# An attention and maxout kernel: loads and turns moved along a hand-written loop, and two output tiles moved ahead of a values step

## The chip, the core and the metric

The kernel runs on one core of one Trainium2 chip. The core has a matrix engine (TensorE, PE in the profile, with its weight loads shown as PEld), three other compute engines (VectorE is DVE, ScalarE is ACT, GpSimd is POOL), a queue engine (SyncE, SP) and 16 DMA engines. Each engine works through its own list of instructions in order and waits on semaphores for the others. The metric is the device time of one execution in microseconds (us).

## The reference

Two computations follow one another. The first is causal attention with 16 extra keys and values ("beacons") ahead of the sequence, for 8 batches, 8 heads, 576 tokens and head size 64. The second is a feed-forward layer that takes the largest of three products, on 4608 rows of 512.

```python
k_all = np.concatenate([beacon_k, k], axis=2)
v_all = np.concatenate([beacon_v, v], axis=2)
scores = scale * np.matmul(q, k_all.transpose(0, 1, 3, 2))
scores = np.where(causal, -1000000000.0, scores)
a = np.exp(scores - scores.max(-1, keepdims=True))
a /= a.sum(-1, keepdims=True) + 1e-09
attn_out = np.matmul(a, v_all)
x = attn_out.transpose(0, 2, 1, 3).reshape(B * S, H * D)
h = np.maximum(np.maximum(x @ w1, x @ w2), x @ w3)
out = h @ w_out
```

## The kernel before, in words

Attention is worked by pairs of heads, 32 pairs in all: four pairs to a batch, two pairs to a quad. For a pair, q and k are loaded in float32 into a staging tile `st` (eight buffers), cast to bf16 by POOL ("cast", L259), and turned so that the head dimension lies on partitions. From pair 14 on the turn is a DMA transpose, one for q and one for k ("cross", L378), into one of six pairs of tiles `qT` and `kT`; pairs before are turned by TensorE. "keys" copies the beacons' columns into `kT`. The values of a batch come in two pieces, loaded into `st` and cast into `v_sb`.

For each pair there are four groups of scores ("scores", L513): two or four matmuls into a PSUM tile, an exponential on ACT into `at_sb` (L522), and a causal mask on POOL ("mask", L541). When two pairs (a quad) are masked, a "values" step (L582) multiplies the weights with `v_sb` and with ones, for the first and for the second half of the tokens, 120 matmuls in all. ACT turns the sums into reciprocals ("invert", L603 and L605), DVE multiplies into `xT` ("multiply", L615), and POOL copies the other half into `xC` ("cross x", L680). A batch has two such values steps.

The feed-forward layer runs by blocks of tokens, one block to a batch after the first, one batch behind attention. A "unit" (L699) is 16 matmuls for one weight matrix and one slice of 128 hidden features. DVE takes the larger value into `hT` (L629, L631). "out" (L725) is the second layer for one or two tiles of 128 tokens, six matmuls a tile, with a copy to `y` by DVE (L733) and a store from SP (L759).

The order is a list of steps written out by hand (`first_steps`, `loop_steps`), which `emit_all` runs one after the other, so it is the order of every engine's instructions as well. In the loop one scores step and one unit alternate on TensorE, so that ACT and POOL work while units run. Four PSUM tiles, numbers 0 to 3, serve all steps; the last number of a step names its tile.

The step "load" takes the next entry of the list `loads` (pair loads and value pieces, in a fixed order) and issues its transfers from SP. With an engine's name it is gated: `load_pair` and `load_v` first let that engine write one column of the staging tile, so that the transfer waits until the engine has come to this place. All transfers of SP (loads, turns, stores) stand in one queue in program order.

```python
def next_load(n=1, gate=None):
    for _ in range(n):
        if loads:
            loads.pop(0)(*([idle[gate]] if gate else []))
```

Of the kernel before, what the change touches and what calls it, by code (L numbers as in the profile page):

```python
# [16 lines left out]
def kernel(  # L17
# [160 lines left out]
    def L(fn, *a):  # L178
        return lambda *more: fn(*a, *more)
# [656 lines left out]
    def start_late():  # L836
# [224 lines left out]
        ("load", 1, "pool"),  # L1061
        ("scores", 7, 3, 0),
        ("load", 1),
# [57 lines left out]
        ("cast", 12, "pool", "pool"),  # L1121
        ("load", 1),
        ("load", 1),
        ("scores", 9, 3, 0, 3),
        ("mask", 9, 3, "pool"),
        ("unit", 1),
        ("scores", 9, 1, 0, 0),
# [18 lines left out]
        ("cast", 14, "pool", "pool"),  # L1146
        ("cross", 14, 0),
        ("cross", 14, 1),
        ("load", 1),
        ("unit", 2),  # L1150
# [6 lines left out]
        ("cast keys 2", "pool"),  # L1157
        ("load", 1),
# [3 lines left out]
        ("cross keys",),  # L1162
        ("scores", 11, 2, 0, 0),
        ("mask", 11, 2, "pool"),
        ("unit", 1),
        ("scores", 11, 3, 0, 2),
# [4 lines left out]
        ("unit", 1),  # L1171
        ("unit", 2),
        ("cast", 15, "pool", "pool"),
        ("cross", 15, 0),
        ("cross", 15, 1),
        ("load", 1),
# [9 lines left out]
        ("cast", 16, "pool", "pool"),  # L1186
        ("cross", 16, 0),
        ("cross", 16, 1),
        ("load", 1),
# [6 lines left out]
        ("out", 2, 1),  # L1196
        ("store", 1),
        ("out", 1, 2),
        ("store", 1),
        ("scores", 12, 0, 0, 3),  # L1200
        ("mask", 12, 0, "pool"),
        ("unit", 0),
        ("load", 1),
        ("cast v", 3, 0, "pool"),
        ("scores", 12, 2, 0, 1),
        ("mask", 12, 2, "pool"),
        ("unit", 2),
        ("keys", 14, "act"),
        ("scores", 12, 3, 0, 3),
        ("mask", 12, 3, "pool"),  # L1210
        ("unit", 0),
        ("cast v", 3, 1, "pool"),
        ("scores", 12, 1, 0, 1),
        ("mask", 12, 1, "pool"),
        ("unit", 2),
        ("scores", 13, 0, 0, 3),
        ("mask", 13, 0, "pool"),
        ("unit", 0),
        ("cast", 17, "pool", "pool"),
        ("cross", 17, 0),  # L1220
        ("cross", 17, 1),
        ("load", 1),
        ("scores", 13, 2, 0, 1),
        ("mask", 13, 2, "pool"),
        ("unit", 2),
        ("keys", 15, "act"),
        ("scores", 13, 3, 0, 3),
        ("mask", 13, 3, "pool"),
        ("unit", 0),
        ("scores", 13, 1, 0, 1),  # L1230
        ("mask", 13, 1, "pool"),
        ("unit", 2),
        ("scores", 14, 0, 0, 3),
        ("mask", 14, 0, "pool"),
        ("unit", 0),
        ("cast", 18, "pool", "pool"),
        ("cross", 18, 0),
        ("cross", 18, 1),
        ("load", 1),
        ("scores", 14, 2, 0, 1),  # L1240
        ("mask", 14, 2, "pool"),
        ("unit", 2),
        ("keys", 16, "act"),
# [11 lines left out]
        ("unit", 3),  # L1255
        ("scores", 14, 1, 0, 2),
        ("mask", 14, 1, "pool"),
        ("unit", 0),
        ("cast", 19, "pool", "pool"),
        ("cross", 19, 0),  # L1260
        ("cross", 19, 1),
        ("load", 1),
# [3 lines left out]
        ("keys", 17, "act"),  # L1266
        ("scores", 15, 2, 0, 2),
        ("mask", 15, 2, "pool"),
        ("unit", 0),
        ("scores", 15, 3, 0, 1),  # L1270
# [5 lines left out]
        ("load", 1, "pool"),  # L1276
# [8 lines left out]
        ("cross x", 2, 1, 1, "pool"),  # L1285
        ("cast", 20, "pool", "pool"),
        ("cross", 20, 0),
        ("cross", 20, 1),
        ("load", 1),
        ("out", 2, 0),  # L1290
        ("store", 1),
        ("out", 2, 1),
        ("store", 1),
        ("scores", 16, 0, 0, 3),
        ("mask", 16, 0, "pool"),
        ("unit", 2),
        ("load", 1),
        ("cast v", 4, 0, "pool"),
        ("scores", 16, 2, 0, 0),
        ("mask", 16, 2, "pool"),  # L1300
        ("unit", 3),
        ("keys", 18, "act"),
        ("scores", 16, 3, 0, 1),
        ("mask", 16, 3, "pool"),
        ("unit", 2),
        ("cast v", 4, 1, "pool"),
        ("scores", 16, 1, 0, 0),
        ("mask", 16, 1, "pool"),
        ("unit", 3),
        ("scores", 17, 0, 0, 1),  # L1310
        ("mask", 17, 0, "pool"),
        ("unit", 2),
        ("cast", 21, "pool", "pool"),
        ("cross", 21, 0),
        ("cross", 21, 1),
        ("load", 1),
        ("scores", 17, 2, 0, 0),
        ("mask", 17, 2, "pool"),
        ("unit", 3),
        ("keys", 19, "act"),  # L1320
        ("scores", 17, 3, 0, 1),
        ("mask", 17, 3, "pool"),
        ("unit", 2),
        ("scores", 17, 1, 0, 0),
        ("mask", 17, 1, "pool"),
        ("unit", 3),
        ("scores", 18, 0, 0, 1),
        ("mask", 18, 0, "pool"),
        ("unit", 2),
        ("cast", 22, "pool", "pool"),  # L1330
        ("cross", 22, 0),
        ("cross", 22, 1),
        ("load", 1),
        ("scores", 18, 2, 0, 0),
        ("mask", 18, 2, "pool"),
        ("unit", 3),
        ("keys", 20, "act"),
        ("values", 8, 0, 1),
# [7 lines left out]
        ("unit", 0),  # L1346
        ("scores", 18, 3, 0, 3),
        ("mask", 18, 3, "pool"),
        ("unit", 1),
        ("scores", 18, 1, 0, 3),  # L1350
        ("mask", 18, 1, "pool"),
        ("unit", 2),
        ("cast", 23, "pool", "pool"),
        ("cross", 23, 0),
        ("cross", 23, 1),
        ("load", 1),
        ("scores", 19, 0, 0, 0),
        ("mask", 19, 0, "pool"),
        ("unit", 1),
        ("keys", 21, "act"),  # L1360
        ("scores", 19, 2, 0, 3),
        ("mask", 19, 2, "pool"),
        ("unit", 2),
        ("scores", 19, 3, 0, 0),
        ("mask", 19, 3, "pool"),
        ("unit", 1),
        ("scores", 19, 1, 0, 3),
        ("mask", 19, 1, "pool"),
        ("unit", 2),
        ("load", 1, "pool"),  # L1370
        ("unit", 0),
        ("values", 9, 0, 1),
        ("invert",),
        ("values", 9, 1, 3),
# [5 lines left out]
        ("cast", 24, "pool", "pool"),  # L1380
        ("cross", 24, 0),
        ("cross", 24, 1),
        ("load", 1),
        ("out", 2, 2),
        ("store", 1),
        ("out", 2, 0),
# [5 lines left out]
        ("unit", 2),  # L1392
        ("load", 1),
        ("cast v", 5, 0, "pool"),
        ("scores", 20, 2, 0, 0),
        ("mask", 20, 2, "pool"),
        ("unit", 1),
        ("keys", 22, "act"),
        ("scores", 20, 3, 0, 3),
        ("mask", 20, 3, "pool"),  # L1400
        ("unit", 2),
        ("cast v", 5, 1, "pool"),
        ("scores", 20, 1, 0, 0),
# [4 lines left out]
        ("unit", 2),  # L1408
        ("cast", 25, "pool", "pool"),
        ("cross", 25, 0),  # L1410
        ("cross", 25, 1),
        ("load", 1),
        ("scores", 21, 2, 0, 0),
        ("mask", 21, 2, "pool"),
        ("unit", 1),
        ("keys", 23, "act"),
        ("scores", 21, 3, 0, 3),
        ("mask", 21, 3, "pool"),
        ("unit", 2),
        ("scores", 21, 1, 0, 0),  # L1420
# [4 lines left out]
        ("unit", 2),  # L1425
        ("cast", 26, "pool", "pool"),
        ("cross", 26, 0),
        ("cross", 26, 1),
        ("load", 1),
        ("scores", 22, 2, 0, 0),  # L1430
        ("mask", 22, 2, "pool"),
        ("unit", 1),
        ("keys", 24, "act"),
        ("values", 10, 0, 3),
# [6 lines left out]
        ("cross x", 4, 0, 1, "pool"),  # L1441
        ("unit", 0),
        ("scores", 22, 3, 0, 1),
        ("mask", 22, 3, "pool"),
        ("unit", 3),
        ("scores", 22, 1, 0, 1),
        ("mask", 22, 1, "pool"),
        ("unit", 2),
        ("cast", 27, "pool", "pool"),
        ("cross", 27, 0),  # L1450
        ("cross", 27, 1),
        ("load", 1),
        ("scores", 23, 0, 0, 0),
        ("mask", 23, 0, "pool"),
        ("unit", 3),
        ("keys", 25, "act"),
        ("scores", 23, 2, 0, 1),
        ("mask", 23, 2, "pool"),
        ("unit", 2),
        ("scores", 23, 3, 0, 0),  # L1460
        ("mask", 23, 3, "pool"),
        ("unit", 3),
        ("scores", 23, 1, 0, 1),
        ("mask", 23, 1, "pool"),
        ("unit", 2),
        ("load", 1, "pool"),
        ("unit", 0),
        ("values", 11, 0, 3),
        ("invert",),
        ("values", 11, 1, 1),  # L1470
# [4 lines left out]
        ("cross x", 4, 1, 1, "pool"),  # L1475
        ("cast", 28, "pool", "pool"),
        ("cross", 28, 0),
        ("cross", 28, 1),
        ("load", 1),
        ("out", 2, 2),  # L1480
        ("store", 1),
        ("out", 2, 0),
        ("store", 1),
        ("scores", 24, 0, 0, 3),
        ("mask", 24, 0, "pool"),
        ("unit", 1),
        ("load", 1),
        ("cast v", 6, 0, "pool"),
        ("scores", 24, 2, 0, 2),
        ("mask", 24, 2, "pool"),  # L1490
        ("unit", 3),
        ("keys", 26, "act"),
        ("scores", 24, 3, 0, 0),
        ("mask", 24, 3, "pool"),
        ("unit", 1),
        ("cast v", 6, 1, "pool"),
        ("scores", 24, 1, 0, 2),
        ("mask", 24, 1, "pool"),
        ("unit", 3),
        ("scores", 25, 0, 0, 0),  # L1500
        ("mask", 25, 0, "pool"),
        ("unit", 1),
        ("cast", 29, "pool", "pool"),
        ("cross", 29, 0),
# [206 lines left out]
```

## Time and profile before

| | |
|---|---|
| median of 3 runs | 290.99 us |
| the three runs | 288.12, 295.52, 290.99 us |
| the profiled execution | 288.71 us |
| its span (first to last instruction of the program) | 286.9 us |
| TensorE's granted clock over the span | 1.00 |
| HBM read and written | 35.13 MB, 9.44 MB |
| transfers by hardware queues (q1) | 39.20 MB, 72.8% of the 16 DMA engines' time |
| POOL cast of a pair's q or k (x44) | 822 ns each |
| DVE copy of two output tiles (x20, some of one tile) | 1090 ns each |

The profile is of one execution. "Busy" is the time in which an engine worked, and "idle before" the time that it stood ahead of a group of instructions, with what ended that idle time. The chain of waits follows the end of the program back, at each step to what released it. "Issue" there is time in which an engine waited for nothing that the profile shows.

### The profile page before, as it was taken

The numbers are of one execution on the slowest core, as the hardware profiler recorded it, in microseconds if no ns is written. First come the engines' busy times: TensorE is split into PE (matmuls) and PEld (weight loads), VectorE is DVE, ScalarE is ACT, GpSimd is POOL, SyncE is SP. The second block draws the span as 40 slices with busy tenths as digits, with TensorE's granted clock in tenths as the row PEclk, the third lists the DMA queues.
The fourth block names the chain that finished last, engine by engine and source line by source line (L and its number), as shares of the span: only waits on it lengthen the run. The fifth ranks groups of instructions, "written<-read, shape, count | busy, mean of one in ns | idle before, by whom it ended". The sixth has DMA issues, their size and how long they took to land.

```text
span 286.9 us, 11693 instructions
## 1 busy us (share of the span) xinstructions
PE 275.5 (96%) x5099; PEld 204.3 (71%) x5099; DVE 177.1 (62%) x331; ACT 155.1 (54%) x249; POOL 140.6 (49%) x280
## 2 busy tenths in 40 slices
PE   7999999899899999999999998989999999999995
PEld 6656777667677577876888476866888478867762
DVE  2455878866566665756666565645666565761654
ACT  3886676877363367734765176624765186624000
POOL 4562228898763187626763396616763173400000
PEclk9999999999999999999999999999999999999999
DMA  9999999989999989889999999899999220003004
GB/s 156 177 166 210 219 238 159 244 198 218 231 185 159 148 167 305 133 156 177 192 218 163 158 162 295 138 185 164 242 214 141 78 110 5 2 3 148 2 2 183
DMA packets 118307, 46.27 MB, mean 161 GB/s; under 512 B 107248, under 2 KB 112880, under 8 KB 118256
## 3 DMA queue, kind: packets, MB, share of 16 engines
q1 hardware_dynamic: 111888, 39.20, 72.8%
q0 software_dynamic: 5808, 6.00, 13.3%
q8 instruction: 40, 0.66, 1.1%
q10 hardware_dynamic: 560, 0.33, 0.4%
q14 instruction: 11, 0.09, 0.1%
HBM read 35.13 MB, written 9.44 MB: 155 GB/s over the span
## 4 chain that ended last, share of the span: by engine, by line
PE 87%; DMA 4%; ACT 3%; issue 2%; POOL 1%; DVE 1%; ACTq 0%; POOLq 0%
PE t L699 44%; PE t L725 16%; PE t L582 11%; PE t L513 6%; DMA quad<-in_k_dram 2%; ACT at_sb L522 2%; PE pv L637 2%; DMA bk<-in_beacon_k_dram 2%; PE sc L513 1%; PE sc L637 1%; PE fps L637 1%; PE t L397 1%; POOL at_sb L541 1%; PE wide L582 1%; PE pv L582 1%
## 5 line engine op out<-in xcount | busy, mean ns | idle before, releaser
L699 PE MATMUL t<-xT,w_sb 64*128 64x288 bf16 (+1 forms) x1008 | 130.5, 285 | 0.9 <-issue 0.9
L699 PE MATMUL t<-xC,wC 64*128 64x288 bf16 (+1 forms) x1008 | 130.3, 285 | 0.0
L522 ACT ACTIVATE at_sb<-t 128x992 bf16<-128x992 f32 (+1 forms) x96 | 82.7, 863 | 54.4 <-PE t L513 46.4
L541 POOL TENSOR_SCALAR_AFFINE_SELECT at_sb<-at_sb 128x256 bf16<-128x256 bf16 (+2 forms) x143 | 53.3, 389 | 61.2 <-ACT at_sb L522 46.4
L631 DVE TENSOR_TENSOR hT<-hT,t 128x576 bf16<-128x576 bf16 (+1 forms) x84 | 63.7, 762 | 31.3 <-PE t L699 31.3
L699 PEld LDWEIGHTS <-w_sb 64*128 64x128 bf16 x1008 | 52.7, 94 | 12.8 <-issue 2.1
L699 PEld LDWEIGHTS <-wC 64*128 64x128 bf16 x1008 | 52.7, 94 | 11.3
L725 PE MATMUL t<-w_out_sb,hT 128*128 128x512 bf16 x210 | 46.9, 380 | 0.0
L259 POOL CAST p<-st 96x768 bf16<-96x768 f32 x44 | 35.0, 822 | 8.0 <-DMA qT<-p 7.4
L629 DVE CAST hT<-t 128x576 bf16<-128x576 f32 (+1 forms) x36 | 27.7, 769 | 15.2 <-PE t L699 15.0
L615 DVE TENSOR_TENSOR xT<-t,recip 128x288 bf16<-128x288 f32 (+2 forms) x78 | 23.0, 351 | 22.6 <-ACT recip L605 18.9
L725 PEld LDWEIGHTS <-hT 128*128 128x128 bf16 x210 | 19.9, 98 | 23.3 <-issue 0.2
L680 POOL COPY xC<-xT 64x576 bf16<-64x576 bf16 (+1 forms) x26 | 18.2, 699 | 36.1 <-DVE xT L615 35.9
L513 PE MATMUL t<-qT,kT 64*128 64x288 bf16 (+4 forms) x288 | 33.4, 279 | 0.0
L733 DVE COPY y<-t 128x1024 f32<-128x1024 f32 (+1 forms) x20 | 21.8, 1090 | 17.1 <-PE t L725 16.8
L582 PEld LDWEIGHTS <-v_sb 128*32 128x32 bf16 (+1 forms) x1408 | 24.8, 96 | 5.4 <-issue 4.2
L582 PE MATMUL t<-at_sb,v_sb 128*32 128x96 bf16 (+8 forms) x1144 | 24.0, 228 | 3.2 <-issue 3.2
L513 PEld LDWEIGHTS <-kT 64*128 64x128 bf16 x400 | 18.8, 94 | 10.7 <-issue 6.3
L603 ACT ACTIVATE lnd<-t 128x288 f32<-128x288 f32 x26 | 10.7, 410 | 28.7 <-PE t L582 28.7
L522 ACT ACTIVATE at_sb<-sc 128x736 bf16<-128x736 f32 (+5 forms) x28 | 23.2, 862 | 4.3 <-PE sc L513 4.1
L315 POOL CAST v_sb<-st 128x1536 bf16<-128x1536 f32 (+2 forms) x21 | 18.4, 894 | 0.0
L637 PEld LDWEIGHTS <-w_sb 128*128 128x128 bf16 x144 | 13.1, 98 | 3.3 <-issue 1.4
(125 smaller groups left out, 214.2 us busy)
## 6 DMA issues: line engine op xcount, KB each, us to landing
out_dram<-y SPq DMA_DIRECT2D x15, 512.0 KB, 5.3
st<-in_q_dram SPq DMA_DIRECT2D x24, 288.0 KB, 5.8
st<-in_k_dram SPq DMA_DIRECT2D x24, 288.0 KB, 6.6
st<-in_v_dram SPq DMA_DIRECT2D x24, 256.0 KB, 5.4
w_sb<-in_moe_w_dram POOLq DMA_DIRECT2D x6, 384.0 KB, 8.4
st<-in_v_dram SPq DMA_DIRECT2D x8, 224.0 KB, 4.9
st<-in_v_dram SPq DMA_DIRECT2D x8, 160.0 KB, 5.2
out_dram<-y SPq DMA_DIRECT2D x5, 256.0 KB, 2.7
```

The costliest lines, as they stand in the source:

```text
L259: cast(t16.rearrange("p r h d -> p h r d"), st[0:QP, i * NQ2 : (i + 1) * NQ2].rearrange("p (h r d) -> p h r d", h=2, r=QR),)
L513: nc.tensor.matmul(ps[:, e, off : off + q1 - q0], kT[hs, 128 * t : 128 * t + 128], qT[hs, q0:q1], start=True, stop=True, tile_position=(64 ...
L522: nc.scalar.activation(out=both_heads(p, gi), in_=ps[:, :, 0 : g_width(p, gi)], func=AF.Exp, scale=scale)
L541: nc.gpsimd.affine_select(out=view, in_=view, compare_op=ALU.is_ge, fill=0.0, base=x0, pattern=[[0, 2], [1, hi - lo]], channel_multiplier=-1,)
L582: nc.tensor.matmul(ps[bank][32 * j : 32 * j + 32, lo + q0 - qa : lo + qb - qa], lhsT, at_view(PPQ * quad + j // 2, t, j % 2, q0, qb), star ...
L615: nc.vector.tensor_mul(xT[:, 2 * g + part - 1, c0 + ca : c0 + cb], ps[bank][:, lo : lo + cb - ca], recip[:, ca:cb],)
L629: (by_i or by_dve)(h, ps)
L631: nc.vector.tensor_max(h, h, ps)
L637: nc.tensor.matmul(ps[:, f], w_in[i][:, ct, 128 * (ft + f) : 128 * (ft + f + 1)], xT[:, ct, lo : lo + MID], start=(ct == 0), stop=(ct == n ...
L699: nc.tensor.matmul(ps[:, e], w[own(e), ct, cols], x, start=(ct == 0 and not over), stop=(ct == n_ct - 1 and over), tile_position=(64 * e, 0),)
L725: nc.tensor.matmul(ps[:, u], h_tile(tt + u, ft), w_out_sb[:, ft, :], start=(ft == 0), stop=(ft == n_ft - 1),)
L733: nc.vector.tensor_copy(y[:, 0:n], ps[:, 0:n])
```

## The change

No instruction of the computation is added or taken away. Three things move.

The order of `loads` changes: the pair loads of a batch follow that batch's value pieces, where they ran one pair further ahead.

```diff
     loads = load_pairs(10, 12) + load_v_pieces(2) + load_pairs(12, 16)
-    loads += [L(load_beacons, B_PE, B, bk32)] + load_pairs(16, 17)
+    loads.append(L(load_beacons, B_PE, B, bk32))
     for b in range(3, B):
-        loads += load_v_pieces(b) + load_pairs(PPB * b + 5, min(PPB * b + 9, NPAIR))
+        loads += load_v_pieces(b) + load_pairs(PPB * (b + 1), min(PPB * (b + 2), NPAIR))
```

The steps "load", "cast" and "cross" stand at other places. Two loads leave `first_steps` and come later in the loop; casts and turns come two to three pairs ahead of their scores, where they came four to five ahead; most loads are gated by POOL (16 more small fills there). "cast v" comes one pair later, and the cast of the beacons and its turn move a few steps.

Of the four or five output tiles of a block, which stood behind the batch's second values step, two now stand just ahead of the next batch's first values step. The PSUM tile numbers of most steps change with it. This is the batch of pairs 16 to 19, from the end of the batch ahead (mask steps and all of the lines between are left out where "..." stands):

```diff
         ("values", 7, 1, 2),
         ...
         ("cross x", 2, 1, 1, "pool"),
-        ("cast", 20, "pool", "pool"),
-        ("cross", 20, 0),
-        ("cross", 20, 1),
-        ("load", 1),
-        ("out", 2, 0),
-        ("store", 1),
-        ("out", 2, 1),
-        ("store", 1),
-        ("scores", 16, 0, 0, 3),
-        ("unit", 2),
-        ("load", 1),
-        ("cast v", 4, 0, "pool"),
-        ("scores", 16, 2, 0, 0),
-        ...
-        ("scores", 17, 0, 0, 1),
-        ("unit", 2),
-        ("cast", 21, "pool", "pool"),
-        ...
-        ("scores", 18, 0, 0, 1),
-        ("unit", 2),
-        ("cast", 22, "pool", "pool"),
-        ...
-        ("scores", 18, 2, 0, 0),
-        ("unit", 3),
-        ("keys", 20, "act"),
-        ("values", 8, 0, 1),
+        ("cast", 18, "pool", "pool"),
+        ("cross", 18, 0),
+        ("cross", 18, 1),
+        ("load", 1, None),
+        ("out", 2, 0),
+        ("store", 1),
+        ("scores", 16, 0, 0, 1),
+        ("unit", 3),
+        ("scores", 16, 2, 0, 2),
+        ("unit", 1),
+        ("cast", 19, "pool", "pool"),
+        ("cross", 19, 0),
+        ("cross", 19, 1),
+        ("load", 1, None),
+        ...
+        ("scores", 17, 0, 0, 0),
+        ("unit", 3),
+        ("cast v", 4, 0, "pool"),
+        ("scores", 17, 2, 0, 2),
+        ("unit", 1),
+        ("load", 1, "pool"),
+        ...
+        ("scores", 18, 0, 0, 0),
+        ("unit", 3),
+        ("cast", 20, "pool", "pool"),
+        ("cross", 20, 0),
+        ("cross", 20, 1),
+        ("load", 1, "pool"),
+        ("keys", 19, "act"),
+        ("scores", 18, 2, 0, 2),
+        ("unit", 1),
+        ("out", 2, 0),
+        ("store", 1),
+        ("values", 8, 0, 3),
```

More of the change, by code (lines that the diff above doesn't have):

```diff
@@ L1171 @@
         ("unit", 1),
+        ("load", 1, "pool"),
         ("unit", 2),
[L1173 to L1176, printed above, removed]
+        ("cross keys",),
         ("unit", 3),
@@ L1195 @@
         ("store", 1),
-        ("out", 2, 1),
+        ("out", 1, 1),
         ("store", 1),
-        ("out", 1, 2),
-        ("store", 1),
[L1200 to L1206, printed above, removed]
-        ("unit", 2),
[L1208 to L1212, printed above, removed]
@@ L1230 @@
[L1230 to L1243, printed above, removed]
+        ("scores", 12, 0, 0, 2),
+        ("mask", 12, 0, "pool"),
+        ("unit", 3),
@@ L1244 @@
+        ("cross", 16, 1),
+        ("load", 1, "pool"),
+        ("keys", 15, "act"),
+        ("scores", 14, 2, 0, 0),
+        ("mask", 14, 2, "pool"),
+        ("unit", 1),
+        ("out", 2, 2),
+        ("store", 1),
         ("values", 6, 0, 3),
```

532 lines of the change are left out of this document (271 added, 261 removed).

## The prediction

> **What bounds the kernel now.** I read the page's shares first, then the chain of waits in order of time, then the busy time by windows. On the page:
>
> ```profile
> span 286.9 us, 11693 instructions
> ...
> PE 275.5 (96%) x5099; PEld 204.3 (71%) x5099; DVE 177.1 (62%) x331; ACT 155.1 (54%) x249; POOL 140.6 (49%) x280
> ...
> DMA  9999999989999989889999999899999220003004
> ...
> q8 instruction: 40, 0.66, 1.1%
> ```
>
> TensorE is busy for 275.5 of 286.9 us, and no other engine exceeds 62%. DMA is busy nine tenths of every slice up to about 226 us, so it is the resource with the least room, but nothing waits for it unless TensorE does. Whatever the change gives must therefore be TensorE idle time. The chain of waits (start, length, what; "issue" is time in which nothing that the profile shows was waited for) says where that is after the first 56 us:
>
> ```profile
> 56.09 0.91 issue
> ...
> 77.11 1.28 issue
> ...
> 126.45 5.29 PE t L725 x24
> 131.74 0.32 PE t L513 x4
> 132.05 0.98 PE t L699 x16
> ...
> 140.27 0.98 PE t L699 x16
> ...
> 143.62 2.29 PE t L582 x120
> ...
> 157.17 6.58 PE t L725 x30
> ...
> 175.48 2.29 PE t L582 x120
> 177.77 0.71 PE t L699 x9
> 178.48 0.91 issue
> ...
> 190.22 1.01 issue
> ```
>
> From 56 us on there are four holes, 0.91 + 1.28 + 0.91 + 1.01 = 4.1 us. All lie in or just behind a values step (L582, 120 matmuls in 2.29 us), and no engine or transfer ends them. To see what they have in common I counted TensorE's work between them, with windows cut inside the holes (columns: width, then busy us and instructions of PE, PEld, DVE, ACT, POOL, clock, DMA share, GB/s):
>
> ```profile
> 56.50:77.80 21.30, 20.12 (x383) 13.88 (x383) 14.00 (x22) 14.47 (x24) 17.49 (x25) 1.00 1.10 206
> 77.80:178.90 101.10, 100.09 (x1916) 74.75 (x1915) 63.42 (x105) 55.79 (x90) 58.66 (x112) 1.00 1.05 189
> 178.90:190.70 11.80, 10.83 (x255) 9.37 (x256) 7.70 (x14) 5.91 (x9) 4.85 (x12) 1.00 1.10 147
> ```
>
> Matmuls plus weight loads are 766, 3831 and 511: nearly 3, 15 and 2 times 256 (instructions that only wait are not counted). The page has 40 instruction packets, 0.66 MB, for 2 x 5099 TensorE instructions: 255 instructions a packet. So a packet holds 256 instructions and the holes stand at packet limits. A values step uses 240 instructions in 2.29 us, a first-layer unit (L699) 32 in 0.98 us, four second-layer output tiles (L725) 48 in 5.29 us, so two tiles 24 in 2.64 us. A values step eats nearly a packet in 2.29 us; where the packet limits lie at its two ends, the next packet comes too late. That is my reading of the holes, an inference from counts.
>
> [...]
>
> **The change, part by part.** The sum is made on the profiled execution: 288.71 us, of which 286.9 is span and 1.8 lies around it.
>
> *TensorE's work* is the same: both programs have 5099 matmuls. 0 us.
>
> *Gates.* 16 loads get a tiny fill on POOL ahead of them. The fills there are now (busy us, mean ns, idle before):
>
> ```profile
> L202 POOL MEMSET st<- 96x1 f32 x6 | 0.6, 106 | 0.1
> ```
>
> 16 x 0.106 = 1.7 us on an engine that is 49% busy and that TensorE doesn't wait for: 0 us, 1.7 if that cover were gone. The load behind a gate waits until POOL gets there, and SP with it; queued behind it on SP are the next turn, which waits for a later POOL cast anyway, and the next store, for whose tile there are four buffers.
>
> *Output tiles moved from behind a second values step.* They covered the chain from a values step to the first unit of the next block (reciprocal, multiply, copy into xC). Its last link, and the cast that follows it, on POOL:
>
> ```profile
> 128.49 0.66 POOL L680 COPY xC<-xT 64x576 bf16<-64x576 bf16 x1 [0.89 <-DVE xT L615]
> 129.22 1.59 POOL L259 CAST p<-st 96x768 bf16<-96x768 f32 x2
> ```
>
> The copy ends at 129.15, 2.70 us behind the values step (ended 126.45). With four tiles the first unit stood at 132.05. With two it stands at 126.45 + 2.64 + 0.32 = 129.41, still 0.26 us later than the copy, and only its second half, 0.49 us on, reads that copy. So 0 us; if the copy slipped by a whole microsecond, 1.0 - 0.75 = 0.25 us in each of seven blocks, 1.8 us.
>
> *The same tiles ahead of a first values step* give ACT and POOL 2.64 us more for masks that nobody waits for now: 0 us. They also shift packet limits. Counting instructions in the two programs, the packets of the last two holes hold the same as before: 119 values matmuls then, 120 now; 118 then and now. So these holes can shrink only by faster packets. One packet that was nearly as tight, over the values step at 143.62 (97 values matmuls), gets 12 output matmuls in place of 11 of the units': 2.64 - 11 x 0.98/16 = 2.0 us more room.
>
> *Loads and turns moved.* Two pair loads leave the stretch ahead of 77.11; I take half off that hole (bounds: all 1.28, or nothing). The hole at 56.09 stands ahead of all edits and stays; 178.48 falls in a stretch whose new neighbours (a turn, a V load, a store) are as heavy as its old ones and stays at 0.91; at 190.22 the V load moves away, and I take half of 1.01. Gain 0.64 + 0.50 = 1.1 us, at best 4.1 - 0.9 = 3.2. At worst a loss: the last two holes grow to the longest seen, 1.28, and the two packets that hold 81 and 86 values matmuls and pass now get one each: 0.4 + 0.3 + 2 x 1.28 = 3.2 us. I stay near the rows of the four holes, as DMA stays busy.
>
> What is late next is the turn, cast two to three pairs ahead where it was four to five. For pair 18, cast just behind a second values step: cast at 129.22 as in the row above; its scores stand behind two output tiles and eight steps of scores and unit, 126.45 + 2.64 + (140.27 + 0.98 - 131.74) = 138.6. That is 9.4 us. What a turn takes (casts on POOL, issues on SP, then median us from issue to landing):
>
> ```profile
> 108.01 1.59 POOL L259 CAST p<-st 96x768 bf16<-96x768 f32 x2
> ...
> 112.50 3.28 SPq L378 DMA_TRANSPOSE qT<-p  x1
> 115.89 2.02 SPq L378 DMA_TRANSPOSE kT<-p  x1
> ...
> 128.72 1.22 SPq L378 DMA_TRANSPOSE kT<-p  x1
> ```
>
> ```profile
> qT<-p SPq DMA_TRANSPOSE x16, 5.0
> kT<-p SPq DMA_TRANSPOSE x16, 3.8
> ```
>
> Undelayed: cast to 130.81, the second issue some 1.3 us after the first, so 132.1 + 3.8 = 135.9, 2.7 us to spare. The slowest quoted: cast at 108.01, landed 115.89 + 3.8 = 119.7, 11.7 us, as its first issue came 2.9 us behind the cast's end, held up on SP by earlier transfers; that would be 2.3 us late. In the new order only one pair load, gated some four units earlier, stands ahead of such a turn on SP, so I take the undelayed value: 0 us. Behind a late turn, SP holds the next load and store, and TensorE, in order, everything.
>
> Sum: 288.7 - 1.1 = 287.6. The three timed runs lie at 288.12, 290.99 and 295.52, the profiled one 2.3 us under their median. A scatter of 7 us from waits on a full DMA should partly stay: I put back 1.2 of the 2.3 us, an estimate without a row, and forecast 288.8.
>
> **The rivals.** *A: no packet comes faster.* For: the last turn moves behind seven units with their scores, a values step and three output tiles, 7 x (140.27 + 0.98 - 131.74)/8 + 2.29 + 3.96 = 14.6 us, so the same bytes get 14.6 us more room in some 226, and DMA stays nearly full. The holes stay at 4.1 us. Time: 288.7 to 291.0. [...] Chance 0.20.
>
> *B: the spread works everywhere.* The three holes behind 56.09 close (3.2 us) and the runs lose their scatter: 285.5; with the first hole as well 284.6, the floor, as nothing else from 56 us on is idle. For: where DMA is at 0 to 2 tenths, behind 230 us, no hole stands in a values step. Against: the unmoved counts of the last two packets. Chance 0.23.
>
> *C, slower: turns come late.* Pairs 18, 22, 26 and 30 are cast behind second values steps; each has 9.4 us, or 10.7 where a third tile stands there (22, 30). At the slow turn's 11.7 us TensorE stands 2 x 2.3 + 2 x 1.0 = 6.6 us. It decides from a landing 9.4 us behind the cast. 287.6 + 6.6 = 294.2, and with the median's 2.3 us 296.5. For: DMA is full, and the 16 turns' medians hide such cases. Against: SP's queue ahead of these turns is shorter. Chance 0.15.
>
> Forecast, partly closed holes and no new wait: 0.42.
>
> **How the numbers follow.** The time is the likeliest case's, 288.8, whose own range is 286.5 to 291. The whole range takes in B's floor, 284.6, and most of C, up to 294.5. About 2% is what this kernel's runs can tell from no change, 285.2 to 296.8. Faster: B's lower part and the edge of the forecast, 0.22. Slower: C with a bad median, or C with new holes (3.2 us), 0.13. The rest, 0.65.
>
> **What would show it.** In the changed profile the chain should have TensorE's steps back to back from 56 us on, with "issue" holes only in or behind values steps and multiples of 256 instructions apart; the one near 178 us should be there still. Two tiles after a second values step must be followed by scores and unit with no gap. A gap ahead of scores ended by the transfer of qT or kT is C, and makes the prediction wrong; so do more than four holes, or none.

## The result, and the profile after

| | kernel before | changed kernel |
|---|---|---|
| median | 289.54 us (22 runs, 287.30 to 295.52) | 287.55 us (22 runs, 286.11 to 290.53) |
| the profiled execution | 288.71 us | 289.68 us |
| ratio | | 0.9936, 95% interval 0.9915 to 0.9957 |

The change makes the kernel 0.6% faster, 2.0 us by the medians. The ratios here and below leave out the runs that are more than 1.5% above the fastest of the same kernel, while the medians and the counts of runs take in all. The profiled execution of the changed kernel is one of its slowest, so its profile tells where time can go and not what the median gained. A second profile of the same kernel, taken later beside other kernels, is of 288.82 us.

The page of the changed kernel, the lines that answer to those shown of before:

```profile
span 287.9 us, 11732 instructions
...
PE 277.3 (96%) x5099; PEld 204.6 (71%) x5099; DVE 177.2 (62%) x331; ACT 155.0 (54%) x249; POOL 142.9 (50%) x296
...
DMA  9999997999979299999999999997999551003004
...
q8 instruction: 40, 0.66, 1.0%
```

The same 5099 matmuls and 40 packets; POOL is 2.3 us busier; DMA is at seven tenths or more in all slices up to 223 us but one, and at five tenths or less behind. The chain of waits of the changed kernel (start, length, what):

```profile
60.30 2.76 PE t L725 x12
...
76.70 1.78 PE t L582 x83
78.54 0.70 PE t L582 x37
...
126.70 2.70 PE t L725 x12
...
129.72 0.98 PE t L699 x16
...
141.28 2.70 PE t L725 x12
...
155.24 1.86 PE t L582 x86
157.22 0.68 PE t L582 x31
...
176.32 2.29 PE t L582 x120
178.61 1.09 PE t L699 x16
...
187.58 2.28 PE t L582 x116
189.86 1.26 issue
...
213.77 0.71 issue
...
284.68 0.36 DVE y L751
```

A hole inside a step shows as two rows of that step whose times don't meet: 76.70 + 1.78 = 78.48 against 78.54, so 0.06 us where 1.28 us stood before; 155.24 + 1.86 = 157.10 against 157.22, so 0.12 us, new. The hole that stood at 178.48 is gone (176.32 + 2.29 = 178.61). The one at 190 is there and longer, 1.26 us, and there is a new one at 213.77, 0.71 us. From the first pair of output tiles at 60.30 on that is 2.15 us, where the kernel before has 1.28 + 0.91 + 1.01 = 3.20 us.

The same rows at the two ends, in the chain of the kernel before and in that of the second profile of the changed kernel:

```profile
59.00 2.70 PE t L725 x12
...
283.69 0.36 DVE y L751
```

```profile
59.44 2.69 PE t L725 x12
...
188.91 1.27 issue
...
212.84 0.76 issue
...
283.80 0.36 DVE y L751
```

From the first tiles to the last copy the kernel before takes 283.69 - 59.00 = 224.69 us, the changed one 224.38 and 224.36 us. So in the profiled executions the holes give 1.0 us and the whole stretch gives only 0.3. Most of the other 0.7 us is the price of taking a step of output tiles apart: 24 matmuls in 5.29 us before, 2 x 2.70 us now, which is 0.11 us in each of the five blocks that are split, 0.55 us. The run with little DMA traffic shows the same 0.11 us below.

None of this is 2 us. A part of that gain must lie in executions of the kernel before that are not its profiled one; the last two experiments bear on it.

### The profile page after: what moved, and what is told of

Its sections match the earlier page's. It is cut to its first block, busy times and chain, and to the rows that moved or that the text cites. A ratio compares the mean times of both kernels' runs of the same rounds, so it can differ in the third digit from the quotient of the medians.

```text
span 287.9 us, 11732 instructions
## 1 busy us (share of the span) xinstructions
PE 277.3 (96%) x5099; PEld 204.6 (71%) x5099; DVE 177.2 (62%) x331; ACT 155.0 (54%) x249; POOL 142.9 (50%) x296
## 4 chain that ended last, share of the span: by engine, by line
PE 85%; DMA 7%; issue 4%; POOL 1%; DVE 1%; POOLq 0%; DVEq 0%
PE t L699 44%; PE t L725 16%; PE t L582 10%; PE t L513 6%; DMA w_out_sb<-in_moe_w_out_dram 5%; DMA st<-in_v_dram 3%; PE pv L477 2%; PE pv L582 1%; PE sc L513 1%; PE t L397 1%; PE fps L637 1%; POOL at_sb L541 1%; PE sc L477 1%; POOL v_sb L315 1%; PE fps L582 0%
## 5 line engine op out<-in xcount | busy, mean ns | idle before, releaser
L541 POOL TENSOR_SCALAR_AFFINE_SELECT at_sb<-at_sb 128x256 bf16<-128x256 bf16 (+2 forms) x143 | 54.3, 396 | 51.3 <-ACT at_sb L522 42.3
L699 PEld LDWEIGHTS <-wC 64*128 64x128 bf16 x1008 | 52.1, 94 | 11.4
L725 PE MATMUL t<-w_out_sb,hT 128*128 128x512 bf16 x210 | 47.7, 380 | 0.1
L582 PEld LDWEIGHTS <-ones 128*32 128x32 bf16 (+2 forms) x512 | 11.0, 95 | 7.3 <-issue 4.4
```

Of the source, the lines that this page charges most:

```text
L541: nc.gpsimd.affine_select(out=view, in_=view, compare_op=ALU.is_ge, fill=0.0, base=x0, pattern=[[0, 2], [1, hi - lo]], channel_multiplier=-1,)
L582: nc.tensor.matmul(ps[bank][32 * j : 32 * j + 32, lo + q0 - qa : lo + qb - qa], lhsT, at_view(PPQ * quad + j // 2, t, j % 2, q0, qb), star ...
L699: nc.tensor.matmul(ps[:, e], w[own(e), ct, cols], x, start=(ct == 0 and not over), stop=(ct == n_ct - 1 and over), tile_position=(64 * e, 0),)
L725: nc.tensor.matmul(ps[:, u], h_tile(tt + u, ft), w_out_sb[:, ft, :], start=(ft == 0), stop=(ft == n_ft - 1),)
```

## The experiments

My theory: TensorE loses time where a packet of 256 instructions comes too late behind a dense values step, and the change moves some packets. The first rival: the holes have nothing to do with packet limits. The second: one part of the change does all of it. Each ratio below is to the kernel before on the same chip in the same session, with its 95% interval.

**One part alone: the tiles.** The output tiles stand as in the changed kernel; loads, casts, turns and the list of loads are as before.

```diff
-    loads.append(L(load_beacons, B_PE, B, bk32))
+    loads += [L(load_beacons, B_PE, B, bk32)] + load_pairs(16, 17)
     for b in range(3, B):
-        loads += load_v_pieces(b) + load_pairs(PPB * (b + 1), min(PPB * (b + 2), NPAIR))
+        loads += load_v_pieces(b) + load_pairs(PPB * b + 5, min(PPB * b + 9, NPAIR))
```

> Only the output tiles move (with the PSUM tile numbers that go with it); loads, casts and turns keep their old places. Packet theory: two output tiles (12 matmuls in 2.70 us) ahead of a first values step let TensorE's queue reach the packet limit long before the values matmuls run, so the next packet is there in time. Expected: no hole at the values step near 176 us, the hole near 190 us stays (about 1 us), the hole near 77 us stays (its two loads are back); ratio to the kernel before 0.994 to 0.997. Rival, spread of DMA: the gain comes from loads and turns, so this kernel stays at 0.999 to 1.001 with all four holes.

Measured: 0.9957 (0.9922 to 0.9992). The profiled execution, of 290.93 us, gives the most telling trace of the study. Its chain of waits, and its busy time by windows (columns: width, then busy us and instructions of PE, PEld, DVE, ACT and POOL, the granted clock, DMA share, GB/s):

```profile
77.52 2.44 issue
79.95 1.19 PE t L582 x36
```

```profile
80.00:82.00 2.00, 2.00 (x45) 1.41 (x46) 0.00 (x0) 0.79 (x3) 0.00 (x0) 0.50 0.79 240
82.00:84.00 2.00, 2.00 (x26) 1.28 (x24) 1.39 (x4) 0.89 (x2) 0.89 (x2) 0.75 0.81 181
84.00:90.00 6.00, 6.00 (x94) 4.22 (x92) 3.96 (x6) 3.67 (x5) 4.10 (x9) 1.00 1.47 191
```

The hole in the values step at 77 us is here 2.44 us long, and behind it the granted clock is 0.50, then 0.75, then 1.00 again. A late packet was thus paid twice here, by the hole and by slow matmuls behind it: 36 of the values step took 1.19 us, where 37 took 0.70 us in the changed kernel (the row at 78.54). This execution's mean clock is 0.994, and so is that of three more of this kernel's 12 runs. At 178 us there is no hole, and the one near 190 us stays (0.93 us at 192.31), both as expected. By the medians of all runs, 288.39 and 289.16 us, the ratio is 0.997, at the upper end of what was expected.

**The other part alone: loads and turns.** They stand as in the changed kernel, the tiles as before.

```diff
         ("out", 2, 0),
         ("store", 1),
-        ("scores", 16, 0, 0, 1),
+        ("out", 2, 1),
+        ("store", 1),
+        ("scores", 16, 0, 0, 3),
...
-        ("out", 2, 0),
-        ("store", 1),
-        ("values", 8, 0, 3),
+        ("values", 8, 0, 1),
```

> Only loads, casts and turns move; the output tiles stay behind the second values steps. Packet theory: the holes near 178 and 190 us stay (0.7 to 1.3 us each), the hole near 77 us shrinks below 0.5; ratio 0.997 to 1.000. Spread of DMA: both late holes shrink below 0.5 us; ratio 0.993 to 0.996.

Measured: 0.9966 (0.9939 to 0.9992). Its chain:

```profile
76.30 0.67 issue
177.41 0.62 issue
188.86 0.46 issue
211.97 0.53 issue
```

The hole at 178 us is back with the old place of the tiles, shorter than the 0.91 us of before. Neither expectation had it right: by the packet theory the two late holes, 0.62 and 0.46 us, were to stay at 0.7 us or more and the one at 76.30 to be under 0.5; by the other the late ones were both to be under 0.5. The two ratios' intervals overlap with each other and with that of the whole change: these two runs don't divide the gain.

**Packet limits moved, three ways.** The early part has idle matmuls that keep TensorE busy. Another number of them, of another width so that they take about the same time, moves all packet limits behind them; the rest is the changed kernel. The three versions:

```diff
-        ("busy", 31, 174),
+        ("busy", 46, 117),
```

> The changed kernel with 46 warm-up matmuls of 117 columns in place of 31 of 174 at the start: the same columns, 30 TensorE instructions more, so every packet limit falls 30 instructions earlier in the work. No packet then holds more than 113 values matmuls together with less than 12 output matmuls; the shortest takes 3.5 us of matmuls (values step near 188 us) where it took 2.8. Packet theory: the hole near 190 us shrinks from 1.26 to 0 to 0.6 us, holes from 60 us on sum to under 1 us; ratio 0.988 to 0.992. Rival (the holes belong to the place, that is to the transfers under way there): the hole near 190 us stays at 1 us or more and the ratio is that of the changed kernel, 0.994.

```diff
-        ("busy", 31, 174),
+        ("busy", 22, 245),
```

> The changed kernel with 22 warm-up matmuls of 245 columns in place of 31 of 174: 18 TensorE instructions fewer, so packet limits fall 18 instructions later in the work. The packet at quad 11's values step (near 188 us) then begins behind the step's start less and holds 7 of the output matmuls behind it; quad 12's step is split in two. Packet theory: holes near 190 and 214 us below 0.6 us each, new small ones (under 0.6) near 77 and 157 us; ratio 0.988 to 0.993. Rival (place, not packet): holes near 190 and 214 stay as in the changed kernel, ratio 0.994.

```diff
-        ("busy", 31, 174),
+        ("busy", 50, 108),
...
-        ("busy", 12, 213),
+        ("busy", 31, 82),
```

> The changed kernel with 50 warm-up matmuls of 108 columns and 31 of 82 in place of 31 of 174 and 12 of 213: 76 TensorE instructions more. The packets that hold 118 to 120 values matmuls now lie at the values steps of quads 5, 12 and 13 (near 91, 209 and 221 us); the one near 188 us now holds 80. Packet theory: holes of about 1 us near 93 and 223 us, both at second values steps behind units; none near 190 us, and none at quad 12, a first values step behind two output tiles; ratio 0.994 to 0.999. Rival: the hole stays near 190 us.

Measured: 0.9920 (0.9888 to 0.9951), 0.9958 (0.9911 to 1.0005) and 1.0154 (1.0114 to 1.0194). In none of the three is there a hole near 190 us, the most regular one of the changed kernel. Nothing but the idle matmuls, and with them the limits, moved. The count along TensorE's queue settles more: in all fourteen profiles of this document's kernels, before and after among them, there are 30 holes of 0.4 us or more behind 55 us that no engine and no transfer ended. The first instruction behind each of them, counted from the start of TensorE's list, leaves a remainder of 184 to 195 when divided by 256, also where the limits were moved. So the first rival falls. But other holes took the place of the one near 190 us. In the first version they are 0.55, 0.74, 0.54 and 1.11 us, 2.9 us in all where I had expected less than 1, though its ratio lies in the range expected. In the second there are two early ones of 1.40 and 1.35 us, and one of 0.64 us at 213.19 where less than 0.6 was expected. The third, expected at 0.994 to 0.999, is 1.5% slower. Its chain:

```profile
61.95 3.20 issue
...
227.25 0.93 issue
```

The late hole stands in a second values step, where it was expected; the one expected near 93 us did not come, and the first, of 3.20 us, was not foreseen. Behind that hole the clock is 0.53 from 67 to 69 us. Moving the limits moves the holes; where the next long one will stand I could not predict.

**A third place for output tiles.** Of the two tiles that the changed kernel has ahead of a first values step, one moves to just ahead of a second one, in each block from quad 7 on.

```diff
-        ("values", 7, 0, 3),
+        ("out", 1, 3),
+        ("store", 1),
+        ("values", 7, 0, 2),
...
-        ("out", 2, 0),
+        ("out", 1, 1),
         ("store", 1),
-        ("values", 8, 0, 3),
+        ("values", 8, 0, 2),
```

> The changed kernel with one output tile of each block ahead of the second values step too (from quad 7 on), so one, two or three, and one tile stand in the three places. Packet theory: the tile ahead of the values step of quad 11 closes or halves the hole near 190 us (1.26 us there); one tile ahead of quad 10's step may give back a hole of up to 0.4 near 178; ratio 0.989 to 0.993. Rival: the hole near 190 us stays above 0.8 us, and the tile ahead of a second values step waits for the last unit's maximum on DVE, a new gap of 0.2 to 0.8 us in four places; ratio 0.994 to 1.000.

Measured: 0.9949 (0.9911 to 0.9988), one hole of 1.45 us at 211.02 and none at 190. The hole ahead of which a slow tile now stands is gone, as expected, the one near 211 us is longer than the changed kernel's 0.71 us there, and the time doesn't fall.

**Little DMA traffic.** The loads, casts and turns of pairs 20 to 31 are left out of the changed kernel; TensorE's instructions and all packet limits stay. These lines stand in each of the three functions that load, cast and turn a pair.

```diff
+        if p >= 20:
+            return
```

> The changed kernel without the loads, casts and turns of pairs 20 to 31 (their scores use the q and k of earlier pairs). TensorE's work is the same, DMA carries only value loads and stores from about 140 us on. Theory that a packet is late because DMA is full: no hole near 190 or 214 us (below 0.2 us), though the packet limits stand where they stood; span shorter by 1.5 to 2.5 us than the changed kernel's. Theory that a packet's time is fixed and only the number of instructions between limits counts: the hole near 190 us stays at 0.8 us or more.

Measured: 0.9870 (0.9822 to 0.9917). The rows of its page and of its chain:

```profile
DMA  8999997999979299995462306302351302004004
...
56.57 0.32 issue
142.24 2.29 PE t L588 x116
...
174.21 2.29 PE t L588 x119
```

From about 128 us on (slice 19 of 7.1 us) the DMA engines are at 0 to 6 tenths. There no packet is late, though the limits and the values steps (L588 here) are those of the changed kernel with its holes at 190 and 214 us. That speaks for both being needed, a limit at a dense step and busy DMA engines, as far as one profile can; the last experiment has a profile in which two late holes are gone with the DMA engines full. The rows also give the price of the split tiles with no hole near: from one batch's first values step to the next batch's 174.21 - 142.24 = 31.97 us, where the kernel before has 175.48 - 143.62 = 31.86 us in the same block. That is 0.11 us for the block.

**Turns later.** Casts and turns of pairs 18, 22, 26 and 30 move closer to their scores, behind the first scores of the pair ahead, and so behind the turn of the pair that follows.

```diff
-        ("cast", 18, "pool", "pool"),
-        ("cross", 18, 0),
-        ("cross", 18, 1),
-        ("load", 1, None),
...
         ("scores", 17, 0, 0, 0),
         ("mask", 17, 0, "pool"),
         ("unit", 3),
+        ("cast", 18, "pool", "pool"),
+        ("cross", 18, 0),
+        ("cross", 18, 1),
+        ("load", 1, None),
```

> The changed kernel with the casts and turns of pairs 18, 22, 26 and 30 four steps later (behind the first scores of the pair ahead), so that about 3 us are left from cast to scores where 9.3 to 10.6 were. The rival of late turns: a turn lands 4.9 us or more behind its cast, so TensorE stands 2 to 4 us ahead of the scores of each of these four pairs, the wait ended by the turn of kT, and the clock falls behind it; ratio 1.02 to 1.06. If turns were hidden anyway (landing sooner when fewer transfers are under way): no such wait, ratio 0.992 to 0.997.

Measured: 1.0454 (1.0392 to 1.0515). TensorE's waits (in all, times, the longest), and two windows:

```profile
PE t L513 <- DMA kT<-p: 12.6, 4, 3.7
```

```profile
141.30:143.00 1.70, 1.70 (x28) 1.51 (x30) 0.32 (x1) 1.22 (x3) 0.18 (x1) 1.00 1.16 233
...
178.00:180.00 2.00, 2.00 (x18) 1.40 (x16) 0.29 (x1) 0.94 (x2) 1.09 (x3) 0.50 1.33 229
```

The four turns that were moved are late, by 2.2 to 3.7 us each, and no other is. So rival C's mechanism is real; the changed kernel's own turns keep clear of it, as a later part shows.

**Three places and other limits.** The version with three places, with the idle matmuls changed so that the shortest packets have a slow tile ahead.

```diff
-        ("busy", 31, 174),
+        ("busy", 21, 257),
```

> The kernel with three places for the output tiles, and the idle fillers of the early part changed (21 matmuls of 257 columns in place of 31 of 174, about the same time), which moves every packet limit behind them by 20 instructions towards the end. Theory (a hole comes where the packet before holds much of a values step with nothing slow ahead of it, while DMA is full): from 56 us on less than 1.5 us of holes in all, against 2.7 us in the changed kernel, none of them longer than 1.0 us; ratio to the kernel before 0.988 to 0.994, that is 0 to 2 us below the changed kernel. Rival (the limits do not matter, holes come where DMA happens to be busy): 2 to 4 us of holes as in the other versions, ratio 0.993 to 0.998, no better than the changed kernel.

**The changed kernel once more**, on the same chip.

> The changed kernel once more, beside the version with three places on the same chip. Theory: holes at the same limits as in its first profile, 0.5 to 1.5 us each near 190 and 214 us, none near 178 us, 2 to 3.5 us from 56 us on in all; ratio 0.991 to 0.996. Rival (holes fall at random where DMA is busy): the two late holes are at other places than near 190 and 214 us.

Measured: 0.9954 (0.9919 to 0.9990), median 287.64 us, against 0.9933 (0.9905 to 0.9960), median 287.49 us. The chain of the version with three places:

```profile
57.17 0.62 issue
59.62 2.70 PE t L725 x12
...
281.58 0.36 DVE y L751
```

From the first tiles on it has no hole at all, and takes 281.58 - 59.62 = 221.96 us, 2.4 us less than the changed kernel's second profile. The theory had its profile right. Yet its 12 runs reach from 286.66 to 290.45 us, and its median is no better. The rival had the time right: a profile without holes is one execution out of many. The changed kernel's own holes came at the same places as in its first profile, so holes near 190 and 214 us are regular there.

**The loads ahead of 77 us, put back and taken alone.** Two kernels, run together. In one the changed kernel gets back the early loads of the kernel before, and three later loads go in exchange. In the other the kernel before takes only its first part, up to the values step near 77 us, from the changed kernel; three loads follow one by one behind it. All else stays as it is. The second one's edit, beside two casts that move by one step:

```diff
-        ("load", 1, "pool"),
         ("scores", 7, 3, 0),
-        ("load", 1),
...
         ("cast v", 2, 0, "pool"),
+        ("load", 1, "pool"),
...
-        ("load", 1),
...
-        ("cast", 12, "pool", "pool"),
-        ("load", 1),
-        ("load", 1),
...
+        ("cast", 12, "pool", "pool"),
+        ("load", 1, "pool"),
...
-        ("load", 1),
+        ("load", 2),
```

> The changed kernel with the loads ahead of the values step near 77 us put back as in the kernel before (five there in place of two; three later ones are left out in exchange). So far 23 of 63 unprofiled or profiled runs of the kernel before have a mean granted clock of 0.994 or less, and 1 of 34 of the changed kernel. Theory (the loads ahead of 77 us make the packet behind that values step late; where its hole passes some 2.4 us the clock falls, and that is most of what the change gives the median): 3 or more of 12 runs at 0.994 or less, a hole of 0.7 us or more near 77 us in the profile, median 0.8 to 1.8 us above the changed kernel's 287.5. Rival (the low clock comes from the tiles or from a later place): at most 1 of 12 runs, median 287 to 288.

> The kernel before with only its first part, up to the values step near 77 us, taken from the changed kernel (two loads ahead of that step in place of five; the three others follow in the next 20 us). Everything behind is as before. Theory (as in the run beside it): at most 1 of 12 runs with a mean granted clock of 0.994 or less, against about 4 of 12 of the kernel before, a hole near 77 us below 0.7 us, ratio to the kernel before 0.993 to 0.997. Rival (the low clock has another place): 3 or more of 12 such runs, ratio 0.998 to 1.002.

Measured: the changed kernel with the early loads back is no faster than the kernel before, 1.0006 (0.9971 to 1.0041), median 289.24 us, and 3 of its 12 runs have a mean clock of 0.994 or less. The kernel before with only its early loads moved has 0.9931 (0.9904 to 0.9959), median 287.29 us, and none of its 6 runs has such a clock. TensorE's waits of the one and of the other:

```profile
PE t L582 <- issue: 3.3, 3, 1.7
```

```profile
PE t L582 <- issue: 0.6, 2, 0.3
```

The longest wait of the first is the hole at 77.57, 1.65 us. In the second the hole at this place is 0.27 us. So moving the early loads gives about the whole of the gain of the median, with the rest as before and with the rest changed; tiles, turns and later loads add nothing that these four kernels can tell. Of my rivals it is the second that holds. Two kernels fit this less well. Loads and turns alone, which have the same early loads as the changed kernel, gave 0.9966 (0.9939 to 0.9992), with a clock of 0.994 in 2 of 12 runs and a hole of 0.67 us at this place; tiles alone, with the early loads of before, gave 0.9957 (0.9922 to 0.9992), though 0.997 by the medians of all runs. Whether the later turns without the tiles take something back wasn't tried by itself.

How the early loads do it is less clear than that they do. Rows of the chain of the kernel before with only its early loads moved:

```profile
59.45 2.70 PE t L725 x12
...
176.10 2.29 PE t L582 x119
...
187.36 2.39 PE t L582 x117
...
282.19 0.36 DVE y L751
```

It takes 222.74 us from the first output tiles (59.45) to the last copy (282.19), 1.95 us less than before. The hole at 77 us gives 1.0 us of that; but the holes at 178 and 190 us, 0.91 and 1.01 us, are gone as well, 100 us behind the edit, with TensorE's order and packet limits as before. No run here shows why.

## Why the prediction was right, and where it was not

The median, 287.55 us, lies in the forecast case's own range and 1.25 us under its time, and the difference is within 2%. The prediction was right in where the gain is: TensorE's idle time at packet limits, the hole at 77.11 among them, with no new wait for a turn. It was wrong in the reason that it gave for that hole, in two of the four holes and in most sizes, and it did not see the fall of the clock. That the time came out so near is in good part luck: errors in both directions offset each other, as the parts below show.

**Packets: right.** All holes stand at packet limits, by the count above; in the changed kernel those at 189.86 and 213.77 are 767 instructions apart, 3 x 256 less one. The three versions with moved limits took the hole at 190 away, and in the profile with light traffic no late one is left. Most limits are crossed without such a hole: in no trace do more than four of the 40 packets cost 0.4 us or more from 56 us on; each of those costs 0.4 to 3.2 us.

**"I take half off that hole" (77.11): mis-sized.** It fell from 1.28 to 0.06 and 0.29 us in the two profiles. This was taken as one term of 0.64 us among several; it gave 1.0 to 1.2 us, and it is the hole that went down in every profile with the early loads moved. For eight profiles with the same limits I set the time at which the packet before this hole began to be used against the time at which the transfer of the next one began, from the trace's DMA records:

```
                                  limit    transfer   later by   hole
kernel before                     72.11     75.74      3.63 us   1.28
changed, early loads back         72.57     76.54      3.97      1.65
tiles alone (loads as before)     72.65     77.09      4.44      2.44
changed kernel                    73.48     75.65      2.17      0.06
changed kernel, second profile    72.55     74.97      2.42      0.29
before with early loads moved     72.55     74.78      2.22      0.27
loads and turns alone             71.43     73.99      2.55      0.67
three places for tiles            72.09     74.37      2.27      0.12
```

With the loads of before the transfer begins 3.6 to 4.4 us behind the limit; with those of the changed kernel 2.2 to 2.6. In every row the hole ends 2.6 to 3.1 us behind the transfer's begin; in the first 77.11 + 1.28 = 78.39, 2.65 us behind 75.74. The prediction gave as reason that transfers leave the stretch. They don't. The windows from 66 to 77 us of the kernel before and of the changed one:

```profile
66.00:77.00 11.00, 11.00 (x225) 8.05 (x222) 6.66 (x9) 7.28 (x12) 8.78 (x17) 1.00 1.21 198
```

```profile
66.00:77.00 11.00, 11.00 (x182) 7.94 (x183) 7.25 (x9) 7.15 (x11) 9.43 (x20) 1.00 1.10 280
```

More bytes move in it after the change, 280 GB/s against 198. What differs is the order on SP's queue, in its timeline of before and after (start, length, what):

```profile
64.33 4.80 SPq L211 DMA_DIRECT2D st<-in_q_dram  x1
...
70.93 6.89 SPq L759 DMA_DIRECT2D out_dram<-y  x2
```

```profile
64.36 3.50 SPq L759 DMA_DIRECT2D out_dram<-y  x2
70.76 0.34 SPq L211 DMA_DIRECT2D st<-in_q_dram  x1
```

Before, the loads held SP up and the first two stores of the loop were issued from 70.93 on, just when the packet was due. Now they have been issued by 68 us. That these stores hold up the packet is argued from the order, not shown: no run moved them alone.

**What the profile of before could not show.** Its hole of 1.28 us is a mild case. In 28 of 79 runs of the kernel before, with 3 of 12 and 4 of 12 of the two other kernels that have its early loads, the mean clock is 0.994 or less; of the changed kernel in 1 of 34. Over all kernels with the changed kernel's early loads, but for the two that have holes of over 3 us elsewhere (the third version of the limits, and turns later), it is 4 of 92. Of the kernels with the early loads of before, the one such execution with a trace is that of the tiles alone, with its hole of 2.44 us; that in the others too the clock falls behind the hole at 77 us is argued from the counts. In that trace the clock is at 0.50 for 3.41 us (from 79.58 to 82.99); half of that is 1.7 us of work, 0.006 of some 287 us, so 0.994 is one such fall. The medians of the runs of before with and without it are 290.33 and 288.72 us. So about a third of its runs lost some 1.6 us more: 0.6 us on the mean. The rest of the 2 us, some 1.4 us, would be shorter holes, at 77 us and perhaps elsewhere; there are not enough traces to divide it.

**"178.48 ... stays at 0.91": wrong.** It vanished in both profiles. The packet still holds 120 values matmuls, as I had counted, but its successor's transfer began 0.63 us ahead of the limit where it began 1.35 us behind it. I first put that down to the two slow output tiles that now stand ahead of this values step and give the fetch time. With the tiles there, the transfer began 0.6 to 2.6 us ahead of the limit in four profiles (the changed kernel twice, tiles alone, early loads back). But the last experiment speaks against tiles as the only way: with TensorE's order as before the transfer began 0.17 us ahead, and the hole was gone too. What sets the begin of a transfer here stays open.

**"At 190.22 the V load moves away, and I take half of 1.01": wrong.** The hole was 1.26 and 1.27 us. Of "the two packets that hold 81 and 86 values matmuls" one got a hole, 0.71 and 0.76 us. Both lie within the loss that the prediction bounded at 3.2 us. In the profile of the last experiment the hole at 190 is gone with tiles and limits in their old places.

**Tiles moved: "so 0 us", mis-sized.** The cover was there: the copy into xC ended at 129.34 (first row below), the first unit stood at 129.72 with no gap. But the split of the tiles costs 0.11 us a block, which the rows quoted in the prediction could not tell. The blocks split are five, not the "seven" of the prediction, so this is 0.55 us, and its bound of 1.8 us would be 1.25.

**Turns: right.** POOL and SP in the timeline of the changed kernel, and the landing times of kT in the view of that tile:

```profile
128.68 0.66 POOL L680 COPY xC<-xT 64x576 bf16<-64x576 bf16 x1 [0.81 <-DVE xT L615]
129.41 1.59 POOL L259 CAST p<-st 96x768 bf16<-96x768 f32 x2
```

```profile
131.54 1.23 SPq L378 DMA_TRANSPOSE kT<-p  x1
```

```profile
DMA to landing us min/median/max: 2.5/3.9/5.0
```

Pair 18 is cast at 129.41, its second turn is issued at 131.54 and landed at 135.30; its scores stand at 138.73, 9.3 us behind the cast (9.4 were predicted), with 3.4 us to spare (2.7 predicted). TensorE waits for no DMA turn in the whole execution.

**"I put back 1.2 of the 2.3 us": wrong.** No row stood behind this term. The median of three runs of before, 290.99 us, was itself high; of 22 it is 289.54. And the scatter did not stay: the runs with a low clock, its upper part, are nearly gone. The sum without this term, 287.6, is close to what came out by luck: 1.1 us by halved holes were expected of the profiled execution, which gained 0.3 us between the first tiles and the last copy, and the median gained 2.0.

Rival A is out for the median, as the gain is shown. B in its words, "the runs lose their scatter", was nearer to the truth than the forecast in that one respect, though its holes did not close. C did not occur. No version was shown to beat the changed kernel: the best ratio, 0.9920 (0.9888 to 0.9951), overlaps with 0.9933 (0.9905 to 0.9960).

## What to carry to other kernels

Where an engine runs a dense burst of short instructions (here 120 matmuls in 2.29 us), look for idle time that nothing releases and count the instructions between such holes; what helped here was an edit to the loads shortly ahead of one hole, and a part of the change that looks small may carry all of it. A hole in one profile may be the mild case: here it took 1.28 us in that of the kernel before, and 2.44 us, with the clock at 0.50 for 3.41 us, in that of a kernel with the same early loads. So compare the clock of all runs before sizing a term from one trace. And put the early part of a change into the old kernel alone, and the old early part into the new one: these two kernels told what the versions with moved limits did not.

## What the hardware showed beside that

The clock fell to 0.50 at a hole of 2.44 us, in the trace of the tiles alone, stayed there for 3.41 us and was back at 1.00 within 4 us; with the turns late it stayed at 1.00 behind a hole of 3.16 us that ended at 141.28, and fell to 0.50 at one of 3.73 us (the windows above). As it fell at the hole of 2.44 us and not at the longer one of 3.16 us, the length of a hole alone doesn't decide it; what does was not shown.

The begin of a packet's transfer varies more than the time from there on: at 77 us the transfer began 2.2 to 4.4 us behind the limit in the table, and at 178 us up to 2.6 us ahead of it. From there to the first instruction behind a hole it was 2.5 to 3.1 us at 77 and 190 us in the profiles of that table.
